# Local attention and two expert layers on one core: the first eight attention steps in a new order, a third tile's operands prepared late

## Chip, cores and metric

The kernel runs on 1 core of one Trainium2 chip. The metric is the device time of one execution in microseconds: 864.6 as the median of three runs before the change (863.56 to 865.16).

## What is computed

Three stages follow one another. Attention over 2 batches, 8 heads, 768 positions and 64 dimensions keeps, for each position, the 96 positions up to it and the first 8 (global) ones, with a bias linear in the distance. Its output, seen as 1536 tokens by 512, goes through a layer of 4 experts that all see every token, weighted by given probabilities, and then through a layer of 8 experts of which each token takes one.

```python
def _attn_ref(q, k, v, n_global, n_local):
    scores = scale * np.matmul(q, k.transpose(0, 1, 3, 2))
    keep = is_global | is_local
    scores = np.where(keep, scores + bias, -1000000000.0)
    a = np.exp(scores - np.max(scores, axis=-1, keepdims=True))
    a = a / (np.sum(a, axis=-1, keepdims=True) + 1e-09)
    return np.matmul(a, v)

def _moe_ref(x, domain_probs, w1, w2):
    p = domain_probs / (domain_probs.sum(-1, keepdims=True) + 1e-09)
    for e in range(E):
        out += p[:, e:e + 1] * (np.maximum(x @ w1[e], 0.0) @ w2[e])

def _moe2_ref(x, w_gate, w_output_gate, w1, w2):
    e_idx = np.argmax(x @ w_gate, axis=1)
    for e in range(E):
        h = np.maximum(x[mask] @ w1[e], 0.0)
        out[mask] = gate_w[mask, None] * eom[mask, e, None] * (h @ w2[e])
```

The window sizes are run-time inputs. A general form of the attention (`general_attention`) stands in a branch for sizes other than those the fast form is made for; with these inputs it is jumped over.

## The kernel before

**Tiles and steps.** The 1536 positions are 12 tiles of 128. A step `g` is one tile and one pair of heads: tile `g // 4`, pair `g % 4`. The pieces of a step each have a letter in the strings that order them: S scores on TensorE (`att_S`) and the bias and minimum on VectorE, E two exponentials on ScalarE, N the normalisation (`att_N`: a small addition on POOL L309, a reciprocal on VectorE L310, two scalings on POOL L312), T transposes of the result (`att_T`) with a copy `pt` out of PSUM, P the product with the values (`att_PV`). T runs three steps and P four steps behind S. With every second P, x is cast on ScalarE (L389) and its residual is subtracted on VectorE (L391).

**High part and residual.** From tile 2 on, operands are held as two parts: a cast on ScalarE and a subtraction on VectorE or POOL that gives what the cast lost. Tiles 0 and 1 are the first of each batch (they see only themselves) and stay whole. Tile 2 (the constant `FREE`) is the first that needs split keys `kw` (L193, L197, and L235, L237 from tile 1's transposed keys `k32`), queries `qz` (L181, L185) and values `vs` (`prep_v`, L265, L270). `qz` is one buffer: a tile's queries replace those of the tile before it.

**The start.** Steps 0 to 7 (tiles 0 and 1) are written by `att_first`, each by one string of `ORDER_FIRST`; `att_flush` then writes the T and P that are still missing. In these strings K and O are the transposes of the next tile's keys or queries and their residuals, D the loads of a later tile, V the values, W the cast of half of the first weight quarter, F residuals that were put off (`flush_late`). Every engine works its own queue strictly in the order in which the program is written: what stands behind a waiting instruction on the same engine waits too. At step 5 the value that decides the branch is read and a branch hint is set on PE, ACT, DVE and POOL (L864, L865). Behind the flush stands the branch around `general_attention` (L872), on all five engines, and behind it `x_general(0, 0, 2)`, which on SP issues two transfers of x from `xd` that move data only if the general form ran.

**Chunks.** The first expert layer goes through units (a block of tokens, one expert) of eight chunks `(u, m)`: layer 1 (`moe_L1`, L684) into the PSUM bank `ph`, relu and residual h (`moe_h`, L690, L691), and layer 2 of the chunk before (`moe_L2`, L704). The bank `ph` is single: a chunk's layer 1 begins when the h of the chunk before has been read. `STEPS` says how many attention steps a chunk of the first two units takes along, in the order `ORDER_0` and `ORDER_1`; weights are cast on ScalarE (L618) and their residuals subtracted on VectorE and POOL (L620), one half quarter per chunk.

## Time and profile before

| what | value |
|---|---|
| median of three runs | 864.6 us |
| the profiled execution, whole | 869.21 us |
| its span, first to last instruction | 867.4 us |
| TensorE busy | 830.2 us, 96% |
| weight loads on TensorE | 704.9 us, 81% |
| VectorE busy | 549.6 us, 63% |
| ScalarE busy | 425.6 us, 49% |
| POOL busy | 223.3 us, 26% |
| mean granted clock of TensorE | 0.987 |

The profile is of one execution, and its times count from its first instruction. A timeline row gives the start, the duration, the engine, the line, what is written from what, and in brackets the idle time of the engine before it with what ended it. PE is TensorE, PEld its weight loads, DVE VectorE, ACT ScalarE. An engine's name with a q is its sequencer, which takes branches and waits for semaphores. A granted clock of 1.00 is 2.4 GHz, 0.50 is 1.2 GHz. Busy time of TensorE contains matmuls at either clock.

### The profile page before, as it was taken

What the parts mean: (1) busy time and instruction counts of PE and PEld (TensorE: products, weight loads), DVE (VectorE), ACT (ScalarE), POOL (GpSimd) and SP (SyncE); (2) the same over time, 40 slices, a digit from 0 to 9 for tenths busy, and PEclk for the clock granted to TensorE, in tenths of its full rate; (3) what the DMA queues carried; (4) which work ended last, traced back from release to release, by engine and by line L of the source; (5) the groups of instructions that cost most, each with busy time, mean ns of one, the idle gap of its engine ahead of it and who ended that gap; (6) DMA issues with size and microseconds to landing.
All of it is one profiled execution on the core that took longest, in us unless ns stands there. A gap on an engine that the chain in (4) does not pass through costs nothing. (4 is left out here: it accounts for less than half of the span.)

```text
span 867.4 us, 13319 instructions
## 1 busy us (share of the span) xinstructions
PE 830.2 (96%) x4589; PEld 704.9 (81%) x4589; DVE 549.6 (63%) x1252; ACT 425.6 (49%) x928; POOL 223.3 (26%) x309
## 2 busy tenths in 40 slices
PE   6699999899999999999999999999999899999987
PEld 5498988788888888888888888888898788887775
DVE  4688868777776676775654545443675734667970
ACT  5687757655554455544343233222443433656851
POOL 6555536432220120212000000000300321444730
PEclk9699999999999999999999999999999999999999
DMA  9266606540634153313053223342442744456920
GB/s 217 59 168 177 164 26 172 168 134 20 176 102 118 37 149 120 97 48 136 25 158 109 64 94 110 110 133 97 147 159 72 257 163 145 162 194 205 320 91 25
DMA packets 115782, 111.21 MB, mean 128 GB/s; under 512 B 56284, under 2 KB 82908, under 8 KB 115680
## 3 DMA queue, kind: packets, MB, share of 16 engines
q1 hardware_dynamic: 112720, 103.65, 39.8%
q0 software_dynamic: 2960, 6.33, 2.2%
q8 instruction: 49, 0.80, 0.4%
q14 instruction: 53, 0.43, 0.2%
HBM read 112.56 MB, written 7.10 MB: 138 GB/s over the span
## 5 line engine op out<-in xcount | busy, mean ns | idle before, releaser
L684 PE MATMUL ph<-xb,w 128*128 128x512 f32 (+1 forms) x1440 | 291.6, 352 | 4.8 <-DVE h L691 3.3
L704 PE MATMUL po<-w,h 128*128 128x512 f32 x1152 | 285.3, 393 | 0.0
L684 PEld LDWEIGHTS ph<-xb,w 128*128 128x128 f32 x1440 | 232.8, 191 | 40.4 <-DVE h L691 7.0
L704 PEld LDWEIGHTS po<-w,h 128*128 128x128 f32 x1152 | 212.7, 189 | 41.8
L690 ACT ACTIVATE h<-ph 128x512 fp32r<-128x512 f32 (+1 forms) x120 | 61.4, 512 | 210.8 <-PE ph L684 203.5
L691 DVE SCALAR_TENSOR_TENSOR h<-ph,h 128x512 fp32r<-128x512 f32 (+1 forms) x120 | 70.0, 584 | 144.7 <-ACT h L690 144.2
L608 DVE TENSOR_TENSOR w<-raw,w 128x1024 fp32r<-128x1024 f32 x74 | 90.5, 1223 | 14.1 <-ACT w L607 13.9
L607 ACT CAST w<-raw 128x1024 fp32r<-128x1024 f32 x76 | 79.2, 1042 | 0.3
L1168 PE MATMUL po<-dw,hT 128*128 128x512 f32 x240 | 60.4, 402 | 3.0 <-PEq L1381 1.9
L309 POOL TENSOR_SCALAR m<-m 128x2 f32<-128x2 f32 x48 | 18.1, 376 | 171.1 <-ACT st L303 170.8
L1156 PEld LDWEIGHTS qph<-xsA,dw 128*128 128x128 f32 x480 | 58.1, 192 | 1.9 <-DVE dw L669 1.4
L1156 PE MATMUL qph<-xsA,dw 128*128 128x256 f32 x480 | 58.3, 283 | 1.1 <-DVE dw L669 1.1
L1168 PEld LDWEIGHTS po<-dw,hT 128*128 128x128 f32 x240 | 43.7, 188 | 14.3 <-issue 5.1
L312 POOL TENSOR_SCALAR st<-st,m 128x256 f32<-128x256 f32 (+1 forms) x96 | 47.4, 506 | 27.4 <-DVE m L310 25.1
L669 DVE TENSOR_TENSOR dw<-raw,dw 128x512 fp32r<-128x512 f32 x68 | 50.5, 771 | 3.4 <-ACT dw L662 0.7
L303 ACT ACTIVATE st<-st,m 128x256 f32<-128x256 f32 (+1 forms) x96 | 46.3, 484 | 12.2 <-DVE m L296 11.9
L384 DVE TENSOR_TENSOR xs<-x,xs 64x128 f32<-64x128 f32 x128 | 36.1, 282 | 11.8 <-ACT xs L381 9.0
L662 ACT CAST dw<-raw 128x512 fp32r<-128x512 f32 x74 | 43.2, 616 | 0.1
L608 POOL TENSOR_TENSOR w<-raw,w 128x1024 fp32r<-128x1024 f32 x2 | 4.8, 2403 | 145.8 <-PE po L704 141.2
L620 POOL TENSOR_TENSOR w<-raw,w 128x512 fp32r<-128x512 f32 x29 | 39.4, 1363 | 8.3 <-ACT w L618 7.4
L296 DVE CUSTOM_DVE_ANT_0 st<-s,biasN 128x256 f32<-128x256 f32 x80 | 30.5, 419 | 11.5 <-PE s L291 9.2
L394 POOL TENSOR_TENSOR xb<-xs,xb 128x256 fp32r<-128x256 f32 x16 | 12.2, 764 | 99.0 <-ACT xb L393 99.0
(238 smaller groups left out, 1067.7 us busy)
## 6 DMA issues: line engine op xcount, KB each, us to landing
raw<-in_moe_w_dram SPq DMA_DIRECT2D x144, 512.0 KB
rawx<-in_moe_w_dram SPq DMA_DIRECT2D x24, 512.0 KB
xb<-xd SPq DMA_DIRECT2D x12, 512.0 KB
yd<-acc SPq DMA_DIRECT2D x12, 258.0 KB
qn<-in_q_dram SPq DMA_DIRECT2D x10, 256.0 KB
kn<-in_k_dram SPq DMA_DIRECT2D x10, 256.0 KB
vraw<-in_v_dram SPq DMA_DIRECT2D x10, 256.0 KB
vraw<-in_v_dram SPq DMA_DIRECT2D x10, 224.0 KB
```

What stands on the lines that cost most here:

```text
L303: nc.scalar.activation(st[:, j, 0:n], st[:, j, 0:n], AF.Exp, bias=m[:, j:j + 1], scale=-1.0, accum_out=m[:, 2 + j:3 + j])
L312: nc.gpsimd.tensor_scalar(st[:, j, 0:n], st[:, j, 0:n], m[:, 6 + j:7 + j], 1.0, op0=ALU.mult, op1=ALU.mult)
L607: nc.scalar.copy(o[:, 0], a)
L608: (eng or nc.vector).tensor_tensor(o[:, 1], a, o[:, 0].bitcast(F32), op=ALU.subtract)
L662: nc.scalar.copy(o[:, 0, 2 * cp + c], a[:, c])
L669: (eng or nc.vector).tensor_tensor(o[:, 1, 2 * cp + c], a[:, c], o[:, 0, 2 * cp + c].bitcast(F32), op=ALU.subtract)
L684: nc.tensor.matmul(ph[:, 0:N], W[:, a, c, fs], xb[:, c, bb, cs], start=(c == 0 and i == 0), stop=(c == KC - 1 and i == 2))
L690: nc.scalar.activation(h[:, 0, 0:N], ph[:, 0:N], AF.Relu)
L691: nc.vector.scalar_tensor_tensor(out=h[:, 1, 0:N], in0=ph[:, 0:N], scalar=0.0, in1=h[:, 0, 0:N].bitcast(F32), op0=ALU.max, op1=ALU.subtract)
L704: nc.tensor.matmul(po_t[u][t], h[:, a, t * P:(t + 1) * P], W[:, bb, m % 2, :], start=(m == 0 and i == 0), stop=(m == NM - 1 and i == 2))
L1156: nc.tensor.matmul(ph, W[:, a, c, (m % 4) * P:(m % 4) * P + P], xsA[:, bb, c, :], start=(c == 0 and i == 0), stop=(c == KC - 1 and i == 2))
L1168: nc.tensor.matmul(po, hT[:, a, m, t * P:(t + 1) * P], W[:, bb, m % 4, :], start=(m == 0 and i == 0), stop=(m == NM - 1 and i == 2))
```

## The change

Four things change in the order, and no arithmetic does.

1. `ORDER_FIRST` and `ORDER_FLUSH` are written anew. Each step now holds T, S, E, the normalisation of the step before (`n`) and P. The keys and queries of tile 2 are transposed and split in the flush, after the transposes of steps 6 and 7. The part of tile 2's split keys that comes from tile 1's `k32` is a function of its own, `keys_before`, called in steps 3 and 4 (`0` and `1`). The casts of the first weight quarter come at steps 5 and 6 in place of 4 and 5, and POOL writes one row of the bias per step in place of two in each of the first four.
2. Tile 2's values are split at step 11, in a chunk, and no more in the flush. `STEPS` gives the first chunk no step (it had two) and each of the other seven one (they had 1, 1, 1, 1, 1, 0, 0).
3. `x_general(0, 0, 2)` stands inside the branch.
4. The load of the first weight quarter is issued ahead of tile 2's queries and keys. The loads of tile 3 and the casts of the first quarter's second half come behind the first chunk's layer 1; the residual of the first quarter's second piece is VectorE's, no longer POOL's.

```diff
--- before.py
+++ after.py
@@ -228,19 +228,23 @@
 
         def lo():
             los[0]()
-            if t == FREE:
-
-                for cols, src in ((slice(0, PREV), k32[:, t - 1, :, GC:]), (slice(PREV, P), k32[:, t - 1, :, 0:GC])):
-                    for j, r in enumerate(rows):
-                        nc.scalar.copy(o[r, j, :, cols], src[r])
-                    for j, r in enumerate(rows):
-                        nc.vector.tensor_tensor(o[rows[1 - j], j, :, cols], src[r], o[r, j, :, cols].bitcast(F32), op=ALU.subtract)
-            elif qb and t != AFTER_SWAP:
+            if qb and t not in (FREE, AFTER_SWAP):
                 pv = st_t["kw", t - 1]
                 nc.vector.tensor_copy(o[:, :, :, 0:PREV], pv[:, :, :, P + GC:].bitcast(F32))
                 g0 = P if qb == 1 else PREV
                 nc.vector.tensor_copy(o[:, :, :, PREV:P], pv[:, :, :, g0:g0 + GC].bitcast(F32))
         return lo
+
+    def keys_before(i):
+
+        if i == 0:
+            st_t["kw", FREE] = att.tile([P, 2, NP, 2 * P], F32R, tag="kw", name=f"kw{FREE}", bufs=2)
+        o = st_t["kw", FREE]
+        cols, src = ((slice(0, PREV), k32[:, FREE - 1, :, GC:]), (slice(PREV, P), k32[:, FREE - 1, :, 0:GC]))[i]
+        for j, r in enumerate(rows):
+            nc.scalar.copy(o[r, j, :, cols], src[r])
+        for j, r in enumerate(rows):
+            nc.vector.tensor_tensor(o[rows[1 - j], j, :, cols], src[r], o[r, j, :, cols].bitcast(F32), op=ALU.subtract)
 
     def prep_first(p):
 
@@ -472,15 +476,15 @@
     NG = TILES * NP
     LAG = 3
     NA = NG + LAG + 1
-    W_FIRST = {4: (0, 0), 5: (0, 1)}
+    W_FIRST = {5: (0, 0), 6: (0, 1)}
     late = []
     a_next = [0]
     FIRST = 2 * NP
 
     def att_preps(g):
         t, c = divmod(g, NP)
-        k_at, q_at = (1, 2) if t < 2 else (2, 3)
-        if g >= NG or t + 1 == TILES:
+        k_at, q_at = (1, 2) if t + 1 < FREE else (2, 3)
+        if g >= NG or t + 1 in (TILES, FREE):
             return []
         if t + 1 == AFTER_SWAP and c == 0:
             return [prep_before(t + 1)]
@@ -489,7 +493,7 @@
     def att_values(g):
 
         t, c = divmod(g, NP)
-        if c == LAG and t > FREE and g < NG:
+        if c == LAG and t >= FREE and g < NG:
             prep_v(t)
         if g == 1:
             load_v(2)
@@ -531,6 +535,10 @@
             box.pop("e")()
         elif x == "N" and g < NG:
             att_N(g)
+        elif x == "n":
+            att_N(g - 1)
+        elif x in "01":
+            keys_before(int(x))
         elif x == "K":
             box["o"] = att_preps(g)
         elif x == "O":
@@ -542,9 +550,8 @@
             flush_late()
 
 
-    ORDER_FIRST = ("SKETtNODPFWV", "KSWTOPDtFVEN", "TPSKEOWtVNDF", "FTWSVEKOtDNP",
-                   "KSTWtVENPDOF", "TWKSDEtOVNFP", "TKWtVFSEDPON", "STtPKEWONFDV")
-    ORDER_FLUSH = "TPtTTVtFtPPP"
+    ORDER_FIRST = ("SE", "SEnKOV", "SEnKO", "TtSEn0", "TtSEnP1", "TtSEnPW", "TtSEnPW", "TtSEnP")
+    ORDER_FLUSH = "nTtPFKTtPTtOPPQO"
     ORDER_STEP = "TtPVSKEONFD"
 
     def att_first():
@@ -558,20 +565,25 @@
         a_next[0] += 1
 
     def att_flush():
-        n, p, lo = FIRST - LAG, FIRST - LAG - 1, []
+
+        n, p = FIRST - LAG, FIRST - LAG - 1
         for x in ORDER_FLUSH:
             if x == "T":
-                lo.append(att_T(n))
+                lo = att_T(n)
                 n += 1
             elif x == "t":
-                lo.pop(0)()
+                lo()
             elif x == "P":
                 att_PV(p)
                 p += 1
+            elif x in "KQ":
+                klo = (prep_k if x == "K" else prep_q)(FREE)
+            elif x == "O":
+                klo()
             elif x == "F":
                 flush_late()
-            elif x == "V":
-                prep_v(2)
+            elif x == "n":
+                att_N(FIRST - 1)
 
 
 
@@ -616,7 +628,7 @@
         k = a.shape[1] // 2
         a, o = a[:, k * i:k * i + k], o[:, :, k * i:k * i + k]
         nc.scalar.copy(o[:, 0], a)
-        eng = nc.vector if i and (n or half) else nc.gpsimd
+        eng = nc.vector if i else nc.gpsimd
         late.append(lambda: eng.tensor_tensor(o[:, 1], a, o[:, 0].bitcast(F32), op=ALU.subtract))
 
     def w_split(n, half, eng=None):
@@ -834,8 +846,8 @@
         prep_first(0)
         bias_0(0, 2)
         prep_first(1)
+        w_load(0)
         load_qk(2)
-        w_load(0)
 
 
         make_upper_triangular(nc, tri, val=1.0, diag=False)
@@ -854,9 +866,7 @@
             att_first()
             if i < 3:
                 bias_0(2 * i + 2, 2 * i + 4)
-            if i < 4:
-                for h in range(2 * i, 2 * i + 2):
-                    nc.gpsimd.tensor_scalar(biasN[:, h, :], A, slope[h], 1.0, op0=ALU.mult, op1=ALU.mult)
+            nc.gpsimd.tensor_scalar(biasN[:, i, :], A, slope[i], 1.0, op0=ALU.mult, op1=ALU.mult)
             if i == 4:
                 for j in range(2):
                     nc.gpsimd.memset(qz[rows[1 - j], 2 + j].bitcast(F32), 0.0)
@@ -871,7 +881,7 @@
         starting[0] = False
         with tc.If(gen > 0, label="general"):
             general_attention()
-        x_general(0, 0, 2)
+            x_general(0, 0, FREE)
 
 
         NQW = len(quarters)
@@ -896,7 +906,7 @@
             nc.vector.tensor_tensor(pall, pall, psum.to_broadcast([P, TILES, E1]), op=ALU.mult)
 
 
-        STEPS = (2, 1, 1, 1, 1, 1, 0, 0, 0, 0, 1, 1, 1, 1, 1, 0)
+        STEPS = (0, 1, 1, 1, 1, 1, 1, 1, 0, 0, 1, 1, 1, 1, 1, 0)
 
         pool_e = {}
 
@@ -945,10 +955,6 @@
         def chunk(u, m, steps, ahead):
 
             box = {}
-            if u == 0 and m == 0:
-                w_split_part(0, 1, 0)
-                w_split_part(0, 1, 1)
-                late.append(lambda: w_load(2))
             for i in range(steps - 1):
                 for x in ORDER_STEP:
                     att_part(x, a_next[0], box)
@@ -958,6 +964,11 @@
                     box["h"] = moe_L1(u, m)
                 elif x == "H":
                     box.pop("h")()
+                    if u == 0 and m == 0:
+                        w_split_part(0, 1, 0)
+                        w_split_part(0, 1, 1)
+                        late.append(lambda: w_load(2))
+                        late.append(lambda: att_loads(FIRST - 1))
                 elif x == "2":
                     if prev is not None:
                         moe_L2(*prev)
```

Three places of VectorE's queue show how the instructions move. The names carry the step or the tile (pt5: step 5, kw2: keys of tile 2), and L296/L300 are the bias and minimum of a step's scores.

VectorE, steps 4 and 5 of the start, before:

```order
L325 COPY pt1_292<-tp1_291 128x2x128
L310 RECIPROCAL m4_288<-m4_288 128x2
L325 COPY pt2_312<-tp2_311 128x2x128
L296 ISA st5_328,m5_329<-s5_325,first2_99 128x128
L296 ISA m5_329 128x1
L296 ISA st5_328,m5_329<-s5_325,first2_99 128x128
L296 ISA m5_329 128x1
L197 TENSOR_TENSOR kw2_317<-tk2_318,kw2_317 64x4x128 x2
L237 TENSOR_TENSOR kw2_317<-k32_103,kw2_317 64x4x112 x2
L237 TENSOR_TENSOR kw2_317<-k32_103,kw2_317 64x4x16 x2
L310 RECIPROCAL m5_329<-m5_329 128x2
L391 TENSOR_TENSOR xb0_304<-x0_305,xb0_304 64x2x128 x2
```

and with the change:

```order
L314 RECIPROCAL m2_238<-m2_238 128x2
L247 TENSOR_TENSOR kw2_275<-k32_103,kw2_275 64x4x112 x2
L329 COPY pt1_282<-tp1_281 128x2x128
L300 ISA st4_289,m4_290<-s4_286,first2_99 128x128
L300 ISA m4_290 128x1
L300 ISA st4_289,m4_290<-s4_286,first2_99 128x128
L300 ISA m4_290 128x1
L314 RECIPROCAL m3_266<-m3_266 128x2
L247 TENSOR_TENSOR kw2_275<-k32_103,kw2_275 64x4x16 x2
L329 COPY pt2_311<-tp2_310 128x2x128
L300 ISA st5_318,m5_319<-s5_315,first2_99 128x128
L300 ISA m5_319 128x1
```

The residuals of the transposed keys (L197) are gone from here, and those out of `k32` (L237, now L247) stand around step 4 in two pieces, the first ahead of pt1.

VectorE's last rows ahead of the branch, before:

```order
L325 COPY pt5_445<-tp5_444 128x2x128
L325 COPY pt6_453<-tp6_452 128x2x128
L325 COPY pt7_458<-tp7_457 128x2x128
L265 CAST vs2_462<-vraw2_224 128x16x64
L270 TENSOR_TENSOR vs2_462<-vraw2_224,vs2_462 128x8x64
L391 TENSOR_TENSOR xb0_304<-x4_449,xb0_304 64x2x128 x2
L391 TENSOR_TENSOR xb0_304<-x6_472,xb0_304 64x2x128 x2
```

and with the change:

```order
L329 COPY pt5_419<-tp5_418 128x2x128
L632 TENSOR_TENSOR w0_0_334<-raw0_66,w0_0_334 128x512
L329 COPY pt6_436<-tp6_435 128x2x128
L395 TENSOR_TENSOR xb0_299<-x4_423,xb0_299 64x2x128 x2
L329 COPY pt7_447<-tp7_446 128x2x128
L197 TENSOR_TENSOR kw2_275<-tk2_428,kw2_275 64x4x128 x2
L395 TENSOR_TENSOR xb0_299<-x6_453,xb0_299 64x2x128 x2
L185 TENSOR_TENSOR qz_100<-tq2_462,qz_100 64x512 x2
```

The split of tile 2's values (L265, L270) has left; a weight residual, tile 2's key residual (L197) and, directly ahead of the branch, its query residual (L185) have come in.

VectorE's first rows behind the branch, before:

```order
L296 ISA st8_1634,m8_1635<-s8_1629,biasN_98 128x256
L296 ISA m8_1635 128x1
L296 ISA st8_1634,m8_1635<-s8_1629,biasN_98 128x256
L296 ISA m8_1635 128x1
L310 RECIPROCAL m8_1635<-m8_1635 128x2
L620 TENSOR_TENSOR w1_0_1626<-raw1_67,w1_0_1626 128x512
L691 SCALAR_TENSOR_TENSOR h0_0_1663<-ph0_0_1648,h0_0_1663 128x256
```

and with the change:

```order
L703 SCALAR_TENSOR_TENSOR h0_0_1631<-ph0_0_1618,h0_0_1631 128x256
L632 TENSOR_TENSOR w1_0_1634<-raw1_67,w1_0_1634 128x512
L632 TENSOR_TENSOR w0_1_1637<-raw2_68,w0_1_1637 128x512
L703 SCALAR_TENSOR_TENSOR h0_1_1665<-ph0_1_1650,h0_1_1665 128x256
L300 ISA st8_1673,m8_1674<-s8_1668,biasN_98 128x256
```

The scores of step 8 stood ahead of the first chunk's h0_0; now h0_0 comes first.

VectorE from tile 3's key residual on, before:

```order
L197 TENSOR_TENSOR kw3_1710<-tk3_1711,kw3_1710 64x4x128 x2
L240 CAST kw3_1710<-kw2_317 128x8x112
L242 CAST kw3_1710<-kw2_317 128x8x16
L310 RECIPROCAL m10_1707<-m10_1707 128x2
L339 TENSOR_TENSOR pt8_1740<-tp8_1739,pt8_1740 128x512
L691 SCALAR_TENSOR_TENSOR h0_2_1766<-ph0_2_1746,h0_2_1766 128x256
L296 ISA st11_1774,m11_1775<-s11_1769,biasN_98 128x256
L296 ISA m11_1775 128x1
L296 ISA st11_1774,m11_1775<-s11_1769,biasN_98 128x256
L296 ISA m11_1775 128x1
L620 TENSOR_TENSOR w1_1_1696<-raw3_69,w1_1_1696 128x512
L185 TENSOR_TENSOR qz_100<-tq3_1778,qz_100 64x512 x2
```

and with the change, from the same instruction on:

```order
L197 TENSOR_TENSOR kw3_1764<-tk3_1765,kw3_1764 64x4x128 x2
L233 CAST kw3_1764<-kw2_275 128x8x112
L235 CAST kw3_1764<-kw2_275 128x8x16
L314 RECIPROCAL m10_1761<-m10_1761 128x2
L903 TENSOR_REDUCE psum__1617<-pall_93 128x12
L904 TENSOR_SCALAR psum__1617<-psum__1617 128x12
L905 RECIPROCAL psum__1617<-psum__1617 128x12
L906 TENSOR_TENSOR pall_93<-pall_93,psum__1617 128x48
L269 CAST vs2_1795<-vraw2_225 128x16x64
L274 TENSOR_TENSOR vs2_1795<-vraw2_225,vs2_1795 128x8x64
L343 TENSOR_TENSOR pt8_1800<-tp8_1799,pt8_1800 128x512
L703 SCALAR_TENSOR_TENSOR h0_4_1826<-ph0_4_1806,h0_4_1826 128x256
```

Between the key residual (L197) and pt8 there stand now the four operations on the probabilities (L903 to L906) and the split of tile 2's values (L269, L274); in both orders h, step 11's scores, a weight residual and tile 3's query residual (L185) follow pt8.

## Rows read from the trace of the kernel before

**Rows 1.** Stretch 50 to 60: length, busy PE, PEld, DVE, ACT, POOL, clock, DMA share, GB/s

```profile
50.00:60.00 10.00, 10.00 (x82) 9.15 (x82) 8.22 (x24) 9.46 (x23) 5.72 (x10) 1.00 0.84 223
```

**Rows 2.** Timeline of PE: start us, us, line, tile, [idle before <-releaser]

```profile
25.32 0.65 PE L361 MATMUL x<-pt,v 128*64 128x128 f32 x4 [3.55 <-DVE pt L325]
...
35.56 2.32 PE L684 MATMUL ph<-xb,w 128*128 128x256 f32 x12 [1.25 <-DMA xb<-xd]
...
40.47 2.93 PE L684 MATMUL ph<-xb,w 128*128 128x256 f32 x12 [1.09 <-DVE h L691]
```

**Rows 3.** Timeline of DVE, 20 to 59 us, same columns

```profile
20.54 1.39 DVE L197 TENSOR_TENSOR kw<-tk,kw 64x512 fp32r<-64x512 f32 x2
21.96 1.77 DVE L237 TENSOR_TENSOR kw<-k,kw 64x448 fp32r<-64x448 f32 x4
...
25.87 1.39 DVE L185 TENSOR_TENSOR qz<-tq,qz 64x512 fp32r<-64x512 f32 x2
...
32.13 0.68 DVE L265 CAST vs<-vraw 128x1024 fp32r<-128x1024 f32 x1
...
33.46 1.72 DVE L391 TENSOR_TENSOR xb<-x,xb 64x256 fp32r<-64x256 f32 x4
37.32 0.42 DVE L296 CUSTOM_DVE_ANT_0 st<-s,biasN 128x256 f32<-128x256 f32 x1 [2.14 <-DVEq L872]
...
39.39 0.69 DVE L620 TENSOR_TENSOR w<-raw,w 128x512 fp32r<-128x512 f32 x1
40.00 0.42 DVE L691 SCALAR_TENSOR_TENSOR h<-ph,h 128x256 fp32r<-128x256 f32 x1
...
44.29 0.42 DVE L296 CUSTOM_DVE_ANT_0 st<-s,biasN 128x256 f32<-128x256 f32 x1
...
44.98 1.78 DVE L620 TENSOR_TENSOR w<-raw,w 128x512 fp32r<-128x512 f32 x1
...
52.42 1.41 DVE L185 TENSOR_TENSOR qz<-tq,qz 64x512 fp32r<-64x512 f32 x2 [0.48 <-ACT qz L181]
...
57.86 0.18 DVE L893 TENSOR_REDUCE psum__1625<-pall 128x12 f32<-128x48 f32 x1
```

**Rows 4.** The branch's own instructions (L872): durations ns, first and last start us

```profile
L872 DVEq COMPARE_BRANCH  x1: 84/84/84, 34.0 to 34.0; - x1
...
L872 DVEq EVENT_SEMAPHORE  x1: 21/21/21, 37.2 to 37.2; - x1
```

**Rows 5.** Two half microseconds, columns as in rows 1

```profile
36.50:37.00 0.50, 0.50 (x4) 0.50 (x4) 0.00 (x0) 0.00 (x0) 0.00 (x0) 0.50 0.85 119
...
46.50:47.00 0.50, 0.50 (x3) 0.35 (x3) 0.47 (x2) 0.50 (x2) 0.00 (x0) 1.00 0.80 185
```

**Rows 6.** Timeline of PE, 47 to 54 us

```profile
47.39 1.68 PE L684 MATMUL ph<-xb,w 128*128 128x256 f32 x12
...
49.73 1.63 PE L704 MATMUL po<-w,h 128*128 128x512 f32 x6
51.21 0.89 PE L367 MATMUL x<-pt,vs 128*64 128x128 f32 x12
...
52.31 1.67 PE L684 MATMUL ph<-xb,w 128*128 128x256 f32 x12
53.81 0.28 PE L290 MATMUL s<-kw,qz 128*128 128x256 f32 x1
```

**Rows 7.** DVE's groups by shape, 8 to 50 us: busy us, mean ns, idle before

```profile
L325 DVE COPY pt<-tp 128x256 f32<-128x256 f32 x8 | 3.4, 422 | 1.8 <-PE x L361 1.2 <-PE tp L324 0.5
...
L310 DVE RECIPROCAL m<-m 128x2 f32<-128x2 f32 x11 | 1.8, 165 | 9.9 <-POOL m L309 9.8
```

**Rows 8.** ACT's groups by shape, 8 to 50 us, same columns

```profile
L389 ACT CAST xb<-x 64x256 fp32r<-64x256 f32 x8 | 2.9, 364 | 3.8 <-PE x L361 3.7
...
L181 ACT CAST qz<-tq 64x512 fp32r<-64x512 f32 x4 | 2.3, 579 | 0.1
```

**Rows 9.** Timeline of POOL at step 7's normalisation

```profile
29.46 0.72 POOL L312 TENSOR_SCALAR st<-st,m 128x128 f32<-128x128 f32 x2 [0.37 <-DVE m L310]
```

## The prediction

> **What bounds the kernel now.** I read the busy times by stretch first, then the granted clock in half microseconds, the timelines of TensorE and VectorE, the branch's instructions, and last the groups by shape. From 50 us on TensorE is busy all the time at the full clock [rows 1], so an edit of the start is worth only what it moves the point from which TensorE is full with the same work behind it. In the start TensorE is the engine that waits. It stood 3.55 us before the second half of the first tile's PV products, because VectorE was at key parts and operands of tile 2 [rows 2, 3]; its first layer-1 chunk began at 35.56, the second at 40.47 after 1.09 us of waiting for VectorE's h [rows 2]. That h was late because VectorE, its last x subtraction done at 35.18 (33.46 + 1.72), did nothing until 37.32 [rows 3]: its branch around the general attention was decided at 34.0 and the next instruction behind it came at 37.2, 3.2 us later [rows 4]. And the clock was at its lower level, 1.2 GHz, from 36.5 to 46.5 [rows 5]: the chunk at 40.47 took 2.93 us, the one at 52.31 1.67 [rows 2, 6], about 1.75 times less.
>
> **The change, part by part.** I follow VectorE to the h of the first chunk, then TensorE to one common point, the score product of step 12, which began at 53.81 before [rows 6].
>
> *Steps 0 to 7.* Tile 2's key and query residuals (two instructions each, 1.39 and 1.39) leave this stretch on VectorE [rows 3]; the four residuals from the already transposed keys (1.77) stay but come two to three steps earlier. I cost these at nothing: VectorE idled 9.8 us behind POOL's small additions in this part [rows 7], and without that cover they cost up to 1.77. POOL's bias rows, now one per step, are as many as before. So step 7's normalisation, which ended at 29.46 + 0.72 = 30.2 [rows 9], ends 2.8 earlier, at 27.4. VectorE's reciprocal stood some 0.9 before that, at 26.5.
>
> *The flush.* From 26.5 the chain is in the new VectorE order: pt5 0.42; PV5 0.65 at the full clock [rows 2, 7], or 1.1 at the lower (by the factor 1.75); the x cast on ScalarE, two of 0.36, 0.73; the x subtraction 0.86 (half of 1.72); pt7 0.42; PV7 0.65 to 1.1; the x cast 0.73; ScalarE's four query casts, 4 x 0.58 = 2.3 [rows 3, 8]. That is 6.8 to 7.7 us: the casts end at 33.3 to 34.2. The last query residual waits for them, and directly behind it stands the branch. Its 3.2 us [rows 4] then cover the residual (1.39) and the layer-1 chunk on TensorE, and h follows: 33.3 to 34.2, + 3.2, + 0.1, + 0.42 [rows 3] = 37.0 to 37.9. The second chunk begins there; I take **37.5**, against 40.47. Hidden in this: the key residual (1.39) stands beside PV7 and its cast; POOL's weight residual beside the flush.
>
> *The copy of x.* The wait of the first chunk is put down to the DMA xb<-xd [rows 2], but the chunk began at 35.56 and the last x subtraction ended at 35.18: without the copy at most 0.38 goes, and that chunk no longer sets the next. Zero, at most 0.38. SP's loads of quarter 2 and of tile 3 now follow the branch; tile 3's keys are wanted only after step 10's scores (49.4 below) and their buffers come free in the flush, so I cost them at nothing.
>
> *To step 12.* When TensorE began step 12's scores before, it had done layer 1 of chunks 0 to 3 and layer 2 of 0 and 1. In the new order (one step in each of chunks 1 to 7) it has then done two chunks more of each: 2 x 1.50 + 2 x 1.48 = 5.96 [rows 6]. The point equal to 53.81 is 59.8. TensorE's work from the second chunk to there: five layer-1 chunks 7.5, four of layer 2 5.9, two S with transposes 1.7 (0.84 each, 2.34 less 1.50), two bare S about 1.0 (estimate from the same rows), PV8 with T8 and T9 1.5: 17.6. The lower clock held for 6.0 us after 40.47 [rows 5]; I take as much again, which loses 3.0. 37.5 + 20.6 = 58.1: **1.7 gained if TensorE sets the pace.**
>
> It does not. Tile 3's query residual must be written before step 12's scores, and in VectorE's queue the value split of tile 2 (1.33, from 32.13 to 33.46 before) and the four small operations on the probabilities (about 0.2 each, 0.8) now stand ahead of it. From step 10's scores to that residual VectorE took 44.29 to 53.83 before, 9.5 us, 0.48 of it waiting [rows 3]. With the two blocks it is 9.5 - 0.5 + 1.3 + 0.8 = 11.1. If the weight residuals in it go at 0.69, as at 39.39, and not at 1.78 as at 44.98 [rows 3], up to 1.6 less (the second is taken as slower by half of that): 9.5. Step 10's scores end at 37.5 + 8.9 + 3.0 = 49.4 (three chunks of layer 1 4.5, two of layer 2 3.0, three S 1.4). So step 12 starts at 58.9 to 60.5, middle 59.7, against 59.8. **The sum is a gain of 0.1, bounds 0.9 faster and 0.7 slower**, with another 0.45 either way from 37.0 to 37.9. The profiled execution took 869.2 with a span of 867.4; the median of the runs is 4.6 lower. The same difference is put on it: 864.5.
>
> **A rule weighed.** The clock was at the lower level at 36.5 [rows 5], after a stretch whose longest wait of TensorE was 1.25 us before 35.56 [rows 2]; short waits close together were enough. By the Trainium skill ("TensorE: Matmul & The Clock Gate", "HAM oscillation — how this bites in real kernels"), it is long idle gaps that throttle the engine again. By that rule alone the new order's short gaps would leave the clock up, and the sum would be the first rival's. The row speaks against it.
>
> **The rivals.**
> *The clock stays up.* For it: the 3.55 us stop is gone from steps 5 to 7, and the new flush is denser. Against it: the row just weighed, and the wait of some 3 us for h around 34 to 37. Then the second chunk starts at 37.0, step 10 ends at 45.9, and step 12 starts 9.5 to 11.1 later, 55.4 to 57.0: 2.8 to 4.4 gained, 861.0 as the middle.
> *VectorE does not stop at the branch.* The residual then ends 1.39 after 33.3 to 34.2, h at 35.1 to 36.0, 1.9 earlier than in the sum: 862.6. For it: a hint is issued ahead of the branch. Against it: it was there before as well, and the jump passes about as many rows of VectorE's queue as before (some 440). The Trainium skill ("Runtime: NRT & Kernel Launch", "Instruction fetch mechanics") says that a taken branch whose target isn't in the fetched window waits for a fetch; by that rule the 3.2 us come back, and the chance is small.
> *Slower: VectorE's crowd in chunks 3 to 5.* Value split, probabilities, key parts of tile 3 and two weight residuals stand in one queue ahead of step 12, beside POOL's half of the same work. A weight residual there took 1.78 in place of 0.69 [rows 3]. If the value split doubles likewise (+1.3), the chain is 12.4, step 12 starts at 61.8: 2.0 lost, with the later start of 37.9 it is 2.4: 866.6 to 867.0. It decides once the chain takes over 12.1. For it: that TensorE no longer has the slow clock to hide VectorE by then. Against it: the split took 1.33 with POOL busy beside it.
> *The change does nothing by the moved copy* is part of the sum: at most 0.38.
>
> **How the numbers follow.** A measurement of this kernel tells about 0.2% (1.7 us) from no change. The sum, 864.5 with its own range of 863.2 to 865.8, lies within that: 0.45. The clock rival 0.20, the branch rival 0.04, and 0.05 that the steps themselves gain more than 2.8: faster 0.29. The crowd 0.22, and 0.04 that the early key parts are not covered (1.77): slower 0.26. The range reaches to the middle of the clock rival and just past the crowd: 861.0 to 867.2.
>
> **What would show it.** Right: step 7's normalisation ends near 27.4; VectorE idle for over 1.5 us behind its branch; the second layer-1 chunk near 37.5; a wait of TensorE at step 12's scores for VectorE or the query operand, at 59 to 60.5; the clock at the lower level until well past 41. Wrong: the second chunk later than 39 or before 36; no wait at step 12 and a full clock from 40 on (the clock rival); VectorE's chain from step 10 longer than 12 us (the crowd); or any difference that arises after 70 us, since I move nothing there.

## The result, and the profile after

The change makes the kernel slower: 869.34 us (867.12 to 875.88, 14 runs) against 864.74 us (863.16 to 867.01, 14 runs) for the kernel before, ratio 1.0053 with a 95% interval of 1.0037 to 1.0068. That is 4.6 us, and outside the range that was forecast.

The first profile of before came from an execution 4.5 us above its median. So a second profile was taken of both kernels. The profiled execution of after took 869.93 us with a span of 868.1, near its median. From chunk (0,2) to (2,0) the starts differ by 0.9 us at most between before's two profiles, and by 1.5 between after's two. In the table a time is the start of the first layer-1 product of chunk (unit, chunk) in TensorE's timeline, in us.

| chunk | before | before, again | after | after, again |
|---|---|---|---|---|
| (0,0) | 35.56 | 36.05 | 32.25 | 32.80 |
| (0,1) | 40.47 | 41.09 | 38.13 | 38.53 |
| (0,4) | 56.77 | 55.94 | 50.46 | 51.94 |
| (0,5) | 61.37 | 60.56 | 57.18 | 58.66 |
| (1,1) | 74.05 | 73.24 | 73.16 | 74.67 |
| (1,2) | 77.97 | 77.16 | 77.17 | 78.69 |
| (1,3) | 83.05 | 82.25 | 83.54 | 85.06 |
| (1,4) | 87.53 | 86.72 | 88.02 | 89.54 |
| (1,5) | 91.99 | 91.18 | 93.95 | 95.21 |
| (2,0) | 104.79 | 103.99 | 107.09 | 108.37 |

At chunk (1,1) the same steps stand behind both kernels, and there they are level: 73.2 and 74.1 before, 73.2 and 74.7 after. From (1,1) to (2,0) before takes 30.7 in both profiles, after 33.9 and 33.7. So some 3.1 us of the loss arise between 74 and 107 us, where the prediction moved nothing. The rest of the 4.6 has no place in these profiles: both profiled executions of before were slower than the medians of their runs (869.21 against 864.74, 867.02 against 865.82).

The start in after, TensorE's timeline (rows of [rows 2] and [rows 6] answer):

```profile
32.25 1.66 PE L696 MATMUL ph<-xb,w 128*128 128x256 f32 x12 [0.40 <-ACT xb L393]
38.13 2.54 PE L696 MATMUL ph<-xb,w 128*128 128x256 f32 x12 [4.23 <-DVE h L703]
...
55.74 1.22 PE L371 MATMUL x<-pt,vs 128*64 128x128 f32 x11 [1.19 <-DVE pt L343]
...
58.69 0.28 PE L294 MATMUL s<-kw,qz 128*128 128x256 f32 x1
```

VectorE's timeline of the same stretch ([rows 3] answer):

```profile
34.46 1.39 DVE L185 TENSOR_TENSOR qz<-tq,qz 64x512 fp32r<-64x512 f32 x2 [1.55 <-ACTq L882]
37.66 0.42 DVE L703 SCALAR_TENSOR_TENSOR h<-ph,h 128x256 fp32r<-128x256 f32 x1 [1.80 <-ACT w L630]
...
48.81 0.41 DVE L300 CUSTOM_DVE_ANT_0 st<-s,biasN 128x256 f32<-128x256 f32 x1
...
53.48 0.69 DVE L269 CAST vs<-vraw 128x1024 fp32r<-128x1024 f32 x1
54.20 0.77 DVE L274 TENSOR_TENSOR vs<-vraw,vs 128x512 fp32r<-128x512 f32 x1
54.99 0.69 DVE L343 TENSOR_TENSOR pt<-tp,pt 128x512 fp32r<-128x512 f32 x1
...
57.82 1.40 DVE L185 TENSOR_TENSOR qz<-tq,qz 64x512 fp32r<-64x512 f32 x2
```

The query residual at 34.46 waits for ScalarE's four query casts, the last of which ends at 34.43 (32.06 + 2.37); its row names the branch (L882), behind which ScalarE's sequencer came out at 34.5 as well, but in after_noif, without a branch, the residual begins at 34.48 and its row names those casts. The casts in after:

```profile
32.06 2.37 ACT L181 CAST qz<-tq 64x512 fp32r<-64x512 f32 x4
```

VectorE's branch ([rows 4] answer: 34.0 and 37.2 there), and the clock in a stretch on either side of a fall and a rise (columns as in [rows 1]):

```profile
L882 DVEq COMPARE_BRANCH  x1: 84/84/84, 34.5 to 34.5; - x1
L882 DVEq EVENT_SEMAPHORE  x1: 21/21/21, 37.5 to 37.5; - x1
```

```profile
28.00:38.00 10.00, 4.28 (x29) 2.96 (x27) 5.39 (x12) 6.75 (x14) 4.02 (x5) 0.98 0.18 57
39.00:42.00 3.00, 3.00 (x14) 2.90 (x14) 2.23 (x5) 0.89 (x2) 0.82 (x1) 0.50 0.67 182
43.00:60.00 17.00, 15.61 (x114) 13.99 (x114) 13.26 (x36) 13.74 (x34) 10.20 (x15) 1.00 0.60 154
```

VectorE stands 3.0 us behind its branch, as before, and h comes at 37.66. TensorE waits 4.23 us for it, and right behind that its clock is at the lower level, 1.2 GHz, until about 42. In after's second profile the clock was at the lower level already in the first chunk, ahead of the wait; first a stretch of clock, then the first two chunks in TensorE's timeline:

```profile
31.00:38.00 7.00, 4.30 (x18) 3.35 (x16) 3.02 (x6) 5.26 (x11) 1.24 (x2) 0.50 0.25 80
```

```profile
32.80 2.90 PE L696 MATMUL ph<-xb,w 128*128 128x256 f32 x12 [0.40 <-PEq L882]
38.53 2.93 PE L696 MATMUL ph<-xb,w 128*128 128x256 f32 x12 [2.83 <-DVE h L703]
```

Behind 74 us: TensorE's waits from 74 to 110 us, in the second profile of before (none, so the view has its heading alone) and in after:

```profile
engine line waited for: us in total, times, longest us
```

```profile
engine line waited for: us in total, times, longest us
PE x L371 <- DVE xb L395: 1.4, 2, 0.7
PE x L371 <- DVE pt L343: 0.8, 2, 0.4
PE ph L696 <- DVE h L703: 0.4, 1, 0.4
```

These 2.6 us are the greater part of the 3.1. All but the last 0.4, ahead of chunk (1,7), fall into two places. The first is the PV product near 82, behind tile 3's value split (step 15). The durations of VectorE's two value residuals there (minimum, median, maximum), in before and in after:

```profile
L270 DVE TENSOR_TENSOR vs<-vraw,vs x2: 684/688/692, 79.1 to 79.7; 128x512 fp32r<-128x512 f32 x2
```

```profile
L274 DVE TENSOR_TENSOR vs<-vraw,vs x2: 693/1234/1774, 78.5 to 79.1; 128x512 fp32r<-128x512 f32 x2
```

The second residual takes 1.77 in place of 0.69 us: POOL began a weight residual of the same kind at 78.95, 0.2 us ahead of it. Before, POOL's began at 79.75, with VectorE's already under way, and it was POOL's that became long (1.83). By the Trainium skill ("GPSIMD Engine Reference", "1. Specifications") POOL's access to the on-chip memory is shared with VectorE and contends with VectorE's instructions of two such inputs; the trace agrees. Chunk (1,2) takes 6.37 in both profiles of after and 5.1 in both of before.

The second place is the PV product near 92. POOL's timeline in after, then VectorE's, then TensorE's:

```profile
85.10 0.94 POOL L316 TENSOR_SCALAR st<-st,m 128x256 f32<-128x256 f32 x2 [0.52 <-DVE m L314]
89.53 1.29 POOL L632 TENSOR_TENSOR w<-raw,w 128x512 fp32r<-128x512 f32 x1 [3.49 <-ACT pt L335]
90.91 0.21 POOL L313 TENSOR_SCALAR m<-m 128x2 f32<-128x2 f32 x1
```

```profile
91.15 0.17 DVE L314 RECIPROCAL m<-m 128x2 f32<-128x2 f32 x1 [3.71 <-POOL m L313]
91.24 0.84 DVE L395 TENSOR_TENSOR xb<-x,xb 64x256 fp32r<-64x256 f32 x2
```

```profile
92.23 0.24 PE L371 MATMUL x<-pt,vs 128*64 128x128 f32 x1 [0.68 <-DVE xb L395]
```

POOL did nothing for 3.49 us ahead of a weight residual whose cast had ended at 85.39 (ScalarE, 84.77 + 0.62) and whose data had been read by that cast. The releaser that the row names, pt on ScalarE, is only the event that came last. VectorE's queue stood for 3.71 us behind POOL's small addition, and TensorE for 1.07 behind VectorE. In the window of POOL's stop one packet of instructions moved; the queues' packets from 87 to 88 us:

```profile
q1 hardware_dynamic: 316, 0.08, 72.0%
q14 instruction: 1, 0.01, 5.2%
```

### The profile page after: what moved, and what is told of

It reads as the page before. It is cut to its first block, busy times and chain, and to the rows that moved or that the text cites. A ratio compares the mean times of both kernels' runs of the same rounds, so it can differ in the third digit from the quotient of the medians.

```text
span 868.1 us, 13312 instructions
## 1 busy us (share of the span) xinstructions
PE 830.4 (96%) x4589; PEld 702.2 (81%) x4589; DVE 553.7 (64%) x1253; ACT 425.7 (49%) x928; POOL 219.5 (25%) x308
## 5 line engine op out<-in xcount | busy, mean ns | idle before, releaser
L335 ACT CAST pt<-tp 128x512 fp32r<-128x512 f32 x40 | 23.5, 587 | 29.6 <-PE tp L334 29.4
```

## The experiments

Ratios are to the kernel before on the same chip, each with its 95% interval.

**before_again.** No edit.

> The kernel before, unchanged, for a second profile of it. Its first profile came from an execution 4.5 us above the median, and lost PE time between 600 and 700 us (96.2 busy of 100, against 97.8 in the profile of after). Theory A (the loss of after lies in its first 110 us, and the first profile of before is late for reasons of its own): ratio 1.000, PE busy through 80 to 100 us (over 19.9 of 20), and the span some 3 us shorter than that of the first profile. Theory B (the expert stage behind 600 us differs between the two kernels): the new profile loses in 600 to 700 again and before is as late there as in its first profile.

Measured: 0.9993 (0.9976 to 1.001). TensorE was busy through 80 to 100 us (20.00 of 20) and 97.6 of 100 in 600 to 700, where the first profile had 96.2, and the span was 2.2 us shorter (865.2 against 867.4): theory A. The excess of the first profile of before lay there and in its start.

**after_pad5.** POOL's instructions moved by five places.

```diff
             x_general(0, 0, FREE)
+        pad = const.tile([P, 1], F32, name="pad")
+        for _ in range(5):
+            nc.gpsimd.memset(pad, 0.0)
```

> After with five one-element memsets on POOL right behind the branch, where POOL idles from 29.7 to 35.5 us; nothing else. In after POOL stood from 86.04 to 89.53 although the cast that it waits for had ended at 85.39, a packet of instructions moved at 87.28, and VectorE and then TensorE (1.07 us at 92) waited for it. Theory A (POOL stood for its next block of instructions, whose edge lies at a fixed place in its program): the stop comes five instructions earlier, where POOL waits until 84.3 for exponentials anyway, so TensorE's 1.07 us at 92 is gone and the time falls by about 1 us, to 868.3, ratio to before 1.004. Theory B (POOL waited for data or a semaphore): the same instruction still starts 3.5 us late and the time stays at 869.3, ratio 1.0053.

Measured: 1.003 (1.0016 to 1.0043). POOL's timeline at the same instructions:

```profile
85.03 0.22 POOL L313 TENSOR_SCALAR m<-m 128x2 f32<-128x2 f32 x1 [3.99 <-ACT st L307]
85.78 0.95 POOL L316 TENSOR_SCALAR st<-st,m 128x256 f32<-128x256 f32 x2 [0.52 <-DVE m L314]
86.69 1.30 POOL L632 TENSOR_TENSOR w<-raw,w 128x512 fp32r<-128x512 f32 x1
```

The weight residual now follows at once; chunk (1,4) takes 4.46 instead of 5.93. Adding work to POOL removed its stop. And the packet of instructions moved with the program: it went at 77 to 78 us, ahead of an earlier weight residual, for which POOL waits 1.60 us for ScalarE's cast in both kernels. That queue from 77 to 78 us and that residual, in after_pad5, then the residual in after:

```profile
q14 instruction: 1, 0.01, 4.8%
79.62 1.41 POOL L632 TENSOR_TENSOR w<-raw,w 128x512 fp32r<-128x512 f32 x1 [1.60 <-ACT w L630]
```

```profile
78.95 1.42 POOL L632 TENSOR_TENSOR w<-raw,w 128x512 fp32r<-128x512 f32 x1 [1.60 <-ACT w L630]
```

In the four profiles in which POOL stands there for over 3 us (after, after_again, after_vflush, after_steps1) it stands ahead of the same instruction, the 104th of POOL in the trace, which begins 1.4 to 1.5 us behind the end of the packet (in after the packet ends at 87.28 + 0.83 = 88.11, and POOL goes on at 89.53). So the stop hangs on the place in POOL's program and not on data: theory A. The ratio alone could not tell, since its interval overlaps that of after.

**after_steps1 and before_steps0.** The distribution of steps, taken half back in after and put alone into before.

```diff
-        STEPS = (0, 1, 1, 1, 1, 1, 1, 1, 0, 0, 1, 1, 1, 1, 1, 0)
+        STEPS = (1, 1, 1, 1, 1, 1, 1, 0, 0, 0, 1, 1, 1, 1, 1, 0)
```

```diff
-        STEPS = (2, 1, 1, 1, 1, 1, 0, 0, 0, 0, 1, 1, 1, 1, 1, 0)
+        STEPS = (0, 1, 1, 1, 1, 1, 1, 1, 0, 0, 1, 1, 1, 1, 1, 0)
```

> After with step 8 in the first chunk again and no step in the last chunk of the first unit (1,1,1,1,1,1,1,0), so that only the part 'the first chunk without a step' is taken half back. Theory A (the loss is VectorE's backlog of 68 to 84 us, made by the two steps in the last chunks of the first unit: 9.9 us busy of 10 in 70 to 80, against 7.5 before): that stretch eases to under 9, TensorE's 1.1 us at 81 is gone, and the time falls by 1 to 2.5 us, to 867 to 868. Theory B (the loss is made ahead of 60 us by the late operands): step 8 right behind its operands adds work in front of the first h of VectorE, and the time stays or rises by up to 1 us, 869 to 870.5.

> Before with the change's distribution of steps alone (first chunk none, chunks two to eight one each). Theory A (the distribution makes the loss by crowding VectorE and POOL around 70 to 90 us): half or more of the loss is here, 866.5 to 868.5, ratio 1.002 to 1.0045. Theory B (the distribution costs nothing, the late operands and the order of the first eight steps do): 864 to 865, ratio 0.999 to 1.001.

Measured: after_steps1 1.0044 (1.0029 to 1.0059), before_steps0 1.0004 (0.9992 to 1.0017). The distribution alone costs nothing as a sum, theory B of the second. But its trace has both sides: chunk (1,1) starts at 70.20, 3.0 ahead of the second profile of before, and chunk (1,2) then takes 6.38 instead of 5.1. In after_steps1 chunk (1,2) takes 5.07, as theory A had it, but the time did not fall, because POOL's stop became longer and the clock fell behind it:

```profile
84.70 0.94 POOL L316 TENSOR_SCALAR st<-st,m 128x256 f32<-128x256 f32 x2 [0.37 <-PE s L295]
90.15 1.26 POOL L632 TENSOR_TENSOR w<-raw,w 128x512 fp32r<-128x512 f32 x1 [4.50 <-ACT w L630]
```

```profile
92.00:96.00 4.00, 2.79 (x19) 2.68 (x20) 3.14 (x10) 1.24 (x5) 2.46 (x5) 0.64 0.02 4
```

**after_noif and before_noif.** The branch and its hint taken out of both kernels, and with the branch the general attention. The copy of x is left out of both: in after it stood inside the branch, and in before the line behind it went too, so the second expectation below is wrong where it says that the copy stays. The edit in after, without the lines of the hint:

```diff
-        with tc.If(gen > 0, label="general"):
-            general_attention()
-            x_general(0, 0, FREE)
```

> After without the conditional general attention and the copy of x inside it (they do not run on these inputs), so without a branch there and without the jump over some 440 instructions on VectorE; what is computed here is the same. In after the second chunk's layer 1 starts at 38.13, 5.9 us behind the first, because VectorE stands 3.0 us behind its branch (34.5 to 37.5). Theory A (the stop eats what the new order gains): the second chunk starts near 35.2, POOL's stop at 86 is gone or elsewhere, since the jump is gone, and the time falls by 3 to 4.5 us, to 865 to 866.5 against 869.3. Theory B (the gain is lost by VectorE's load in the chunks, whatever the branch does): the second chunk starts earlier but the third and fourth wait longer, chunk (1,1) still starts near 73, and the time falls by at most 1.5 us (POOL's stop).

> Before without the conditional general attention (it does not run on these inputs); the copy of x stays where it is, as a conditional transfer. The counterpart of the run above: what the stop costs the kernel before, whose second chunk starts at 40.5 to 41.1. Theory A (stop and order are independent): before gains as much as after, 2 to 4 us, 862 to 864 on this chip. Theory B (before hides the stop behind the wait of its flush): under 1 us, ratio 0.999 to 1.000; then the new order is worth its time only without the branch.

Measured: 0.9994 (0.998 to 1.0007) and 0.995 (0.9933 to 0.9967). Both gain 0.5 to 0.6%, and without the branch the new kernel is slower than the old one by about as much as with it. So the stop behind the branch is not what sets them apart. That it costs both the same is not shown: in after_noif POOL's stop is gone too (chunk (1,4) 4.47, 1.2 to 1.5 less), and before_noif has lost the copy of x as well. The second chunk of after_noif starts at 36.38, not at 35.2, and chunk (1,1) at 71.34, not near 73: theory A gave the right time for after, for the wrong reason, and neither theory holds in full. before_noif gained a little more than its theory A said (861.65 us, 862 to 864 expected).

**before_steps0_x_in.** The change's distribution of steps and its copy of x alone. Not only the first part is missing, as the expectation has it, but also the late value split of the second part and all of the fourth.

```diff
-        STEPS = (2, 1, 1, 1, 1, 1, 0, 0, 0, 0, 1, 1, 1, 1, 1, 0)
+        STEPS = (0, 1, 1, 1, 1, 1, 1, 1, 0, 0, 1, 1, 1, 1, 1, 0)
         with tc.If(gen > 0, label="general"):
             general_attention()
-        x_general(0, 0, 2)
+            x_general(0, 0, 2)
```

> The change without its first part: before with the new distribution of steps and with the copy of x inside the branch, but with the old order of the first eight steps, the old flush and the third tile's operands at their old place. Theory A (the late operands and the new order make the loss): 865 to 866.3, ratio 0.998 to 1.001, and chunk (1,1) starts 2 to 3 us ahead of after's 73.2. Theory B (the copy of x in the branch makes it): 868 to 869.5, ratio 1.003 to 1.005.

Measured: 0.9991 (0.9977 to 1.0004), theory A. The whole loss comes with what this kernel leaves out: the new order of steps 0 to 7 with tile 2's operands late, the late value split, and the fourth part. Chunk by chunk against the first profile of after: (0,0) starts at 34.35, 2.1 later; (0,1) at 38.22, level with 38.13; (0,1) takes 3.38 instead of 4.93, since the clock is at 1.00 throughout; (0,4) takes 5.35 instead of 6.72; (1,1) starts at 70.14, 3.0 earlier than in after; (1,4) takes 4.46 instead of 5.93. Its timeline of TensorE, and VectorE's branch:

```profile
34.35 2.03 PE L684 MATMUL ph<-xb,w 128*128 128x256 f32 x12 [0.60 <-PEq L872]
38.22 1.68 PE L684 MATMUL ph<-xb,w 128*128 128x256 f32 x12 [1.83 <-DVE h L691]
```

```profile
L872 DVEq COMPARE_BRANCH  x1: 84/84/84, 34.6 to 34.6; - x1
L872 DVEq EVENT_SEMAPHORE  x1: 21/21/21, 37.6 to 37.6; - x1
```

VectorE comes to its branch at 34.6 with the old order and at 34.5 with the new one. The steps end earlier, but the query residual at the flush's end waits for ScalarE's casts and stands right ahead of the branch, so the second chunk gains nothing. The first chunk, 2.1 earlier, only waits longer (4.23 against 1.83). The lower clock follows that wait in this profile, but in after_again it came before it, so the wait is not shown to be its cause.

**after_pad5_steps2.** after_pad5 with two steps in the fifth chunk, none in the eighth.

```diff
-        STEPS = (0, 1, 1, 1, 1, 1, 1, 1, 0, 0, 1, 1, 1, 1, 1, 0)
+        STEPS = (0, 1, 1, 1, 2, 1, 1, 0, 0, 0, 1, 1, 1, 1, 1, 0)
```

> After with the five small memsets and with one step per chunk in chunks two to four, two in the fifth, one in the sixth and seventh and none in the first and the eighth (0,1,1,1,2,1,1,0). In after, before_steps0 and after_pad5 chunk (1,2) takes 1.4 us longer (6.4 against 5.0 from its layer 1 to the next) than in the kernels whose eighth chunk carries no step: the second of VectorE's value residuals at 79.15 stands behind a residual of POOL (1.77 against 0.68 us). Theory A (the step in the eighth chunk brings the two together): that 1.4 us is gone, 867.3 to 867.8, ratio 1.0015 to 1.0025. Theory B (VectorE is full whichever chunk has the step): the two steps in the fifth chunk cost as much there, 868.8, ratio 1.003.

Measured: 1.0086 (1.0066 to 1.0106). Chunk (1,2) took 5.07, so the step in the eighth chunk is what makes tile 3's split long. But from the fourth chunk's layer 1 to the fifth's, with the extra step between them, 12.3 us passed (4.1 in after), and the gain was lost several times over: theory B, and more than it said.

**after_V, after_V_pad5 and before_s0x_V.** The value split later in its step.

```diff
-    ORDER_0 = ("VPTLatDHSKFb2OEN", "LHa2bF")
+    ORDER_0 = ("PTLatDHSKFb2OEVN", "LHa2bF")
```

> After with the value split of a step in the first two units issued behind the step's scores and exponentials and ahead of its normalisation, instead of first. It concerns step 11 (tile 2, chunk (0,4)) and step 15 (tile 3, chunk (1,2)). In after the split of tile 2 (0.69 and 0.77 us on VectorE) stands ahead of pt8 and TensorE waits 1.19 us before 55.74; that of tile 3 (2.38 us, half of it behind a POOL residual) stands ahead of xb and pt11 and TensorE waits 0.69 and 0.39 near 82. Theory A (the moved value split and the step that now meets it are two of the three places of the loss): chunk (0,4) takes 5.4 instead of 6.7, chunk (1,2) 5.1 instead of 6.4, and the time falls by 2 to 2.7 us against after, ratio to before 1.002 to 1.003. Theory B (VectorE is full there and the wait only moves behind the exponentials): both chunks stay within 0.3 of what they take in after, ratio 1.005.

> The kernel above with the five small memsets on POOL as well, which took POOL's stop for instructions out of the way in an earlier run (chunk (1,4) 4.46 instead of 5.93). Theory A (three places make the loss: the value split of tile 2, that of tile 3, POOL's stop, 1.4 us each): 1.4 us less than the kernel above, ratio to before 0.999 to 1.0015. Theory B (something else adds to it later than 110 us): 1.003 or more.

> Before with the new distribution of steps, the copy of x in the branch, and the value split of step 15 moved as in the two kernels above; the first eight steps and the third tile's operands as before. A version that may beat both: theory A (the split of tile 3 meets POOL's residual in every kernel whose eighth chunk carries a step): chunk (1,2) takes 5.1 instead of 6.4 and the time falls by 1.4 us against the same kernel without the move (ratio 0.9991 there), 0.997 to 0.998. Theory B: no difference to it, 0.999.

Measured: 1.0208 (1.0188 to 1.0227), 1.0201 (1.0184 to 1.0219), and 1.0075 (1.0054 to 1.0095) for before_s0x_V, where the kernel without the move had 0.9991. All three expectations missed, with the sign wrong. TensorE's timeline of after_V at the product of step 8:

```profile
58.18 0.31 PE L371 MATMUL x<-pt,vs 128*64 128x128 f32 x2 [3.64 <-DVE vs L269]
59.93 1.33 PE L371 MATMUL x<-pt,vs 128*64 128x128 f32 x10 [1.45 <-POOL vs L274]
```

That product reads the split values themselves, so the split has to be early, not late. Chunk (0,4) took 11.2 us instead of 6.7, chunk (1,2) 10.4. One step ahead of its use the split already stands on TensorE's path; that is where the change put tile 2's when it moved it from the flush to step 11.

**after_again, after_vflush, after_vflush_pad5 and before_steps1_x_in.** after_again has no edit; after_vflush_pad5 adds the memsets above; before_steps1_x_in is before_steps0_x_in with the steps of after_steps1. The edit of after_vflush:

```diff
-        if c == LAG and t >= FREE and g < NG:
+        if c == LAG and t > FREE and g < NG:
             prep_v(t)
...
-    ORDER_FLUSH = "nTtPFKTtPTtOPPQO"
+    ORDER_FLUSH = "nTtPFKTtPTtOPPVFQO"
...
+            elif x == "V":
+                prep_v(FREE)
```

> The kernel after, unchanged, for a second profile on the same chip as the next runs. Theory A (the three places recur in every execution): chunk (0,4) takes 6.7, chunk (1,2) 6.4 and chunk (1,4) 5.5 to 8.5 again, ratio to before 1.003 to 1.005. Theory B (POOL's stop was one execution's accident): chunk (1,4) takes 4.5 and the ratio is the same all the same.

> After with one move undone: tile 2's value split (cast and two residuals) goes back into the flush, ahead of the query cast, where VectorE stood 1.55 us for ScalarE (32.9 to 34.5) and POOL 5.9 us. Theory A (the split in step 11 stands ahead of pt8 and costs 1.4 us there, and in the flush it is covered): chunk (0,4) takes 5.4 instead of 6.7, the second chunk starts no later than 38.6, and the time falls by 1.0 to 1.4 us against after. Theory B (it delays the query residual, the branch and so the second chunk by as much): second chunk at 39.2 or later and no gain.

> The kernel above with the five small memsets on POOL too. Theory A (value split of tile 2, POOL's stop and the step in the eighth chunk explain the loss, the rest is even): 1.0 to 1.5 us less than the kernel above; ratio to before 0.999 to 1.0015, 2.5 to 3 us better than after. Theory B (the lower clock from 38 to 42, behind the wait for VectorE's h, is a part of its own): 1.002 or more, with chunk (0,1) still at 4.9 against 3.4.

> A candidate to beat both: before with the copy of x in the branch and one step in each of the first seven chunks, none in the eighth (1,1,1,1,1,1,1,0). Theory A (no step in the eighth chunk keeps chunk (1,2) at 5.1 instead of 6.4, and one step in the first chunk costs under 1 us): 863.7 to 864.8, ratio 0.997 to 0.999. Theory B (a step in the first chunk holds VectorE behind the branch, as two did): the same as before, 0.9995 to 1.001.

Measured:

| kernel | ratio | (0,1) start | (0,4) takes | (1,2) takes | (1,4) takes |
|---|---|---|---|---|---|
| after_again | 1.0044 (1.0026 to 1.0062) | 38.53 | 6.72 | 6.37 | 5.67 |
| after_vflush | 1.0019 (1.0003 to 1.0035) | 38.12 | 4.96 | 6.40 | 6.21 |
| after_vflush_pad5 | 1.0 (0.9986 to 1.0013) | 39.39 | 5.03 | 6.36 | 4.47 |
| before_steps1_x_in | 0.9972 (0.9959 to 0.9986) | 39.34 | 4.95 | 5.07 | 4.47 |

All three places recur in the second execution of after. Tile 2's split back in the flush, in a gap of VectorE, shortens chunk (0,4) by 1.8 and leaves the second chunk where it was (in after_vflush_pad5 the clock was at the lower level in the first chunk, which took 2.90 us, and the second began at 39.39); the five memsets then take out POOL's stop, and the kernel is level with before. Two small edits, which touch neither the order of the first eight steps nor the late keys and queries, give back what the change lost. In the places theory A holds for both. The medians split otherwise than it said: the first edit gave 3.2 us (869.91 to 866.72, 1.0 to 1.4 expected), the second 0.65 (1.0 to 1.5 expected), together 3.8. The lower clock stays (chunk (0,1) takes 6.05 in after_vflush_pad5), and so does the longer chunk (1,2), so their price is in the even sum. The intervals of each two neighbours, after_again and after_vflush, after_vflush and after_vflush_pad5, overlap; those of the first and the last do not. The places in the trace carry the single steps.

before_steps1_x_in beats both kernels: 863.16 us, 0.28% faster than before. It has the new place of the copy of x, one step in each of the first seven chunks and none in the eighth, and nothing of the first part, the late value split or the fourth part.

## Why the prediction was wrong, point by point

*Steps 0 to 7: right, one size off.* Step 7's normalisation was put at 27.4 and ended at 28.37 (27.10 + 1.27), against 30.2 before. Of the miss, 0.55 us is POOL's two scalings, which took 1.27 instead of 0.72.

*The flush and the branch: right in kind.* Query casts were to end at 33.3 to 34.2 and ended at 34.43; VectorE's stop came back (3.0 against 3.2). The second chunk was put at 37.5, in 37.0 to 37.9, and started at 38.13 and 38.53. What was not seen is that this owes nothing to the new order of the steps: before_steps0 has the second chunk at 38.64 with the old one. It is the two steps less in the first chunk that moved it.

*The copy of x: right where it counts.* It was to give the first chunk 0.38 at most and nothing behind. Between before_steps0 and before_steps0_x_in the first chunk starts 1.6 earlier (35.99, 34.35), the second 0.4, chunk (1,1) 0.06.

*To step 12: right but for 0.2.* Its scores were put at 58.9 to 60.5, and they start at 58.69, and at 60.16 in the second execution; the equal point of before was 59.8, or 0.8 earlier by its second profile. The chain on VectorE from step 10's scores to tile 3's query residual was put at 9.5 to 11.1 and took 10.4 (48.81 to 59.22). Within it I placed the wait at step 12; it came at the product of step 8 (1.19 before 55.74), for which the value split and then pt stand in VectorE's queue. That the crowd would eat the 1.7 us that TensorE's own pace gained was right: with the split back in the flush chunk (0,5) starts at 55.41 instead of 57.18.

*The step that failed* is the one that ended the sum: "an edit of the start is worth only what it moves the point from which TensorE is full with the same work behind it", and with it the last words of the prediction: "any difference that arises after 70 us, since I move nothing there". Two things were moved there, and the sum had them at nothing. The step in the eighth chunk, which I counted as equal work, brought tile 3's value split into POOL's weight residual: 1.28 us in chunk (1,2), read from the chunk, since no run took this alone out of the time. And POOL's program shifted: up to the weight residual behind the stop the trace of after has 104 instructions of POOL where that of before_steps0_x_in, which has no stop, has 105, and the difference is one weight residual (14 against 15), as the fourth part gave one to VectorE. POOL then stopped, by what after_pad5 shows for its next block of instructions, just where VectorE and TensorE hang on it: 1.47 and 1.21 in chunk (1,4). That this one instruction is enough for it was not run. With 0.3 us in chunks (1,6) and (1,7) and 0.1 in (1,1) this is the 3.1 us. The sum carried no term for either, and [rows 1] could not show them. They cover 50 to 60 us alone, where the prediction wrote "from 50 us on": from 100 to 200 us TensorE was busy for 95.6 us in before. And a stretch that is full in the kernel before need not stay full when the queues behind it shift.

*The rivals.* The clock did not stay up: 0.50 from 39 to 42, and in the second execution from 31 to 44, where the row weighed against the rule had spoken for a fall. The branch rival falls with the 3.0 us stop. The slower rival had the crowd in chunks 3 to 5 decide from a chain of 12.1; the chain was 10.4, so it did not decide, and the kernel was slower by another mechanism.

## What to carry to other kernels

A stretch that is full is full by its queues: before writing "nothing moves behind this point", follow the distributed work (here a step in one more chunk) to the next place where two engines hand over to each other. When an edit shifts instructions of an engine that others wait for, look in the new trace for a stop with no open dependency and a packet of instructions in it, and try a few empty instructions before rewriting anything. And an operand's split that feeds TensorE directly belongs in a gap ahead of its use: it cost nothing that shows in the flush, 1.4 to 1.8 us one step ahead of its use, and 4 to 4.5 more at the end of that step.

## What the runs showed of the hardware

POOL stopped in straight-line code, with no branch near, for 3.2 to 4.5 us (after 3.49, after_again 3.23, after_vflush 3.77, after_steps1 4.50), each time ahead of a weight residual. In after one packet of instructions moved at 87 to 88 us in that stop, while the data queue was at work with loads. That the stop is a wait for instructions is inferred from these packets and from its moving with the program. Five small memsets more on POOL removed it in every kernel that had them. The Trainium skill ("Runtime: NRT & Kernel Launch", "Instruction fetch mechanics") says that crossing from one block of instructions to the next is mostly hidden; here chunk (1,4) took 1.2 to 1.8 us longer by it, and 4.0 longer in after_steps1. Why the kernel before has no such stop was not settled.
